# Streamed float32r tiles stored as evens and odds, and read with the halves interleaved

## The chip, the cores and the metric

The kernel runs on one core of a Trainium2 chip. The metric is the device time of one execution in microseconds (us), median of 3 runs. The engines are TensorE (PE; its weight loads are shown apart as PEld), VectorE (DVE), ScalarE (ACT), GpSimd (POOL) and SyncE (SP, which issues the DMAs here).

## The reference

Causal attention for 4 batches of 12 heads, 448 positions and 64 features, followed by a feed-forward block on the 4 x 448 x 768 result:

```python
scores = q @ k.T / sqrt(64);  scores above the diagonal = -1e9      # 448 x 448 per head
attn = exp(scores - max) / (sum + 1e-9);  x = attn @ v              # heads side by side: B x 448 x 768
xn = (x - mean) / sqrt(var + 1e-6) * g_ln
out = x + relu(xn @ w_ch1) @ w_ch2                                  # 768 -> 3072 -> 768
```

All inputs are float32, except that the two weight matrices arrive as 64-bit values whose 32-bit words the kernel loads and converts itself (`raw`, `bits`, `w`).

## The kernel before, in words

**Splitting.** A product of float32 matrices is made of three float32r products: each operand is split into a high part (a float32r rounding) and a low part (the rest), and high x high, high x low and low x high are added in PSUM. So each product of a 128 x 128 weight block with a 128 x 448 tile is three matmuls whose moving operand (`rhs`, the tile that is streamed past the loaded weights) is a float32r tile in SBUF with 448 columns. The streamed tiles are `xh`, `xl` (input of the first layer, `parts`, `gained1`, `gained2`, `apply1`, `apply2`), `hh`, `hl` (hidden activations, in `ffn`), the operands of the last two batches (`x...h`, `x...l`, `h`, `hx`, in class `Pair`) and `kh`, `kl` (keys, `split1` and `split2`), which are streamed for the scores in 112, 224, 336 or 448 columns because of the causal mask. The weights `wh`, `wl` and the queries `qs` are loaded as weights and are not streamed. Every streamed row lies in SBUF in the order of its columns and is read in that order.

**Stages.** Batch 0's attention comes first, with plain float32 scores (`both`). Then the feed-forward of batch 0 (`ffn`, 864 streamed matmuls; in the first layer its tiles have 450 columns, because two columns of g are appended to get the mean's part) runs while the weights are still being converted on ACT and DVE (`convert1`, `convert2`, `split1`, `split2` of weights) and while attention of batches 1 and 2 goes on between its matmuls. Then the feed-forward of batch 1 (864 matmuls of 448 columns) with the attention of batches 2 and 3, and last the feed-forward of batches 2 and 3 together (`Pair`), which forms 7 block products in place of 8 (Strassen's scheme) with 1512 matmuls of 448 columns; the sums that this needs are made on DVE, POOL and ACT.

**Order.** Every operation is first recorded as a task. `Plan.cost` gives each one a price in ns; `Plan.schedule` works out when each result is needed and `Plan.run` then plays the engines' queues with these prices and picks, engine by engine, the task needed first. Moves that may go to ACT or DVE (`either`, `move`) are given to one of them there. The order that comes out is written out and fixed: on the chip each engine runs its list in this order and waits only for what it reads. `MOVES` adds drawn shifts to the needed times of some tasks; they hang on task numbers.

```python
if t.kw["rhs"].dtype == F32R:
    return max(0.4531 * n + 2.5, 60), 220, False
...
if t.engine == "scalar": ...
    return 0.835 * n + (66 if psum else 155 if "scale" in t.kw else 94), 160, False
```

All instructions of the profile bear line 553 (the loop in `Plan.issue` that writes out the order), so tiles tell them apart.

Of the kernel before, what the change touches and what calls it, by code (L numbers as in the profile page):

```python
# [23 lines left out]
P = 128  # L24
C = 112
# [9 lines left out]
SGROUPS = [[(0, 3)], [(0, 0), (0, 2)], [(0, 1), (1, 1)], [(1, 3)], [(1, 0), (1, 2)]]  # L35
RGROUPS = [[3], [0, 2], [1]]
TGROUPS = [[(0, 0)], [(0, 1), (0, 3)], [(0, 2), (1, 2)], [(1, 0)], [(1, 1), (1, 3)]]
HOLE = [-7, 4]
# [5 lines left out]
SLACK, DMA_SLACK = 200, 6000  # L44
CHANGE, TOGETHER = 150, 12000
PASSES, PORT, LEAST, AFTER, URGENT, START = 6, 300, 300, 1500, 5000, 70000
# [42 lines left out]
class View:  # L89
# [12 lines left out]
    def rearrange(self, pattern, **sizes):  # L102
        left, right = (x.split() for x in pattern.replace("(", "( ").replace(")", " )").split("->"))
        assert left[0] == right[0] == "p" and [x for x in left if x not in "()"] == [x for x in right if x not in "()"]
# [22 lines left out]
        return self._new(self.p, self.idx.reshape(shape), lambda t: t.rearrange(pattern, **sizes))  # L127

# [6 lines left out]
    def real(self):  # L135
        t = self.buf.real
        for step in self.path:
            t = step(t)
        return t


# [36 lines left out]
class Plan:  # L178
# [99 lines left out]
    def cost(self, t):  # L278
# [8 lines left out]
        if t.engine == "tensor":  # L287
            if t.kw.get("rhs") is not None and t.kw["rhs"].dtype == BF16:
                return 0.84 * n, 220, False
            if t.method == "transpose":  # L290
                return 0.89 * n if t.ins[0].dtype == F32 else 86, 220, False
            if t.kw["rhs"].dtype == F32R:
                return max(0.4531 * n + 2.5, 60), 220, False
            wide = t.outs[0].p[1] - t.outs[0].p[0] > D and t.kw["rhs"].p[1] - t.kw["rhs"].p[0] > D
            t.mode = "" if wide else "rows" if t.outs[0].p[1] > D + t.outs[0].p[0] else "columns"
            return (1.68 if wide else 0.84) * n + 5 if n > 1 else 100, 220, False
        if t.engine == "scalar":
# [4 lines left out]
            if isinstance(t.kw.get("scale"), View):  # L302
                return 0.835 * n + 188, 160, False
            return 0.835 * n + (66 if psum else 155 if "scale" in t.kw else 94), 160, False
        if t.engine == "gpsimd":
# [3 lines left out]
            if t.method == "tensor_scalar":  # L309
                return 240 + 0.835 * n, 90, True  # L310
            return 2.42 * n + 60 if n > 8 else 1500, 90, bool(sbuf)
        t.here = 85
# [5 lines left out]
        if "accum_out" in t.kw:  # L318
            t.here = 150
        return n / (1.92 if fast else 0.96) + more, t.here + 60, fast or tiny or (len(sbuf) > 1 and not psum)  # L320

# [240 lines left out]
def kernel(ctx, tc, qk, v, w1, w2, g, out):  # L562
# [169 lines left out]
    class Att:  # L732
# [15 lines left out]
        def columns(self):  # L748

            self.parts()  # L750
            for x in (S, S + 1):
                h, l = (t[:, :, x:x + 1].rearrange("p c x -> p (c x)") for t in (self.xh, self.xl))
                nc.vector.tensor_copy(h, g_sb)
                nc.vector.tensor_tensor(out=l, in0=g_sb, in1=h.bitcast(F32), op=ALU.subtract)

        def gained1(self, c):
            kw = dict(out=self.xh[:, c, :S], in0=self.xT[c], scalar1=g_sb[:, c:c + 1], scalar2=1.0, op0=ALU.mult, op1=ALU.mult)
            nc.either(
                ("scalar", "activation", (), dict(
                    out=self.xh[:, c, :S], in_=self.xT[c], func=ACTF.Copy, scale=g_sb[:, c:c + 1],  # L760
                )),
# [3 lines left out]
        def gained2(self, c):  # L765
            nc.vector.scalar_tensor_tensor(
                out=self.xl[:, c, :S], in0=self.xT[c], scalar=g_sb[:, c:c + 1],
                in1=self.xh[:, c, :S].bitcast(F32), op0=ALU.mult, op1=ALU.subtract,
            )
# [11 lines left out]
        def load_v(self, p):  # L781
# [7 lines left out]
            self.t["v", p] = vt  # L789

        def split1(self, p):
            r = self.t["raw", p]
            qs = ap.tile([P, 2, S], F32R, tag="qs", name="qs", bufs=1)
            kh = ap.tile([P, 2, S], F32R, tag="kh", name="kh", bufs=1)
            kl = ap.tile([P, 2, S], F32R, tag="kl", name="kl", bufs=1)
            rq, rk = r[:, 0:2, :], r[:, 2:4, :]
            move(qs, rq)
            move(kh, rk)
            self.t["qk", p] = qs, kh, kl

        def split2(self, p):
            r = self.t.pop(("raw", p))
            qs, kh, kl = self.t["qk", p]
            rq, rk = r[:, 0:2, :], r[:, 2:4, :]
            nc.vector.tensor_tensor(
                out=qs[D:], in0=rq[D:], in1=qs[D:].bitcast(F32), op=ALU.subtract
            )
            nc.gpsimd.tensor_tensor(out=kl, in0=rk, in1=kh.bitcast(F32), op=ALU.subtract)

# [36 lines left out]
        def scores(self, p, grp):  # L846
            pt = ps.tile([C, S], F32, tag="sc", name="sc", bufs=2)
            o = 0
            for h, i in grp:
# [3 lines left out]
                for kk, part in ((kh, 0), (kl, 1)):  # L853
                    nc.tensor.matmul(
                        pt[:, o:o + n], lhsT=qs[:, h, C * i:C * i + C], rhs=kk[:, h, :n],
                        start=(part == 0), stop=(part == 1),
# [184 lines left out]
        def apply1(self, c):  # L1041
            t = self.xg[c % XG]
            self.t["xg", c] = t
            nc.vector.tensor_tensor(
                out=t, in0=self.xT[c], in1=self.t["mb"], op=ALU.subtract
            )
            nc.vector.scalar_tensor_tensor(
                out=t, in0=t, scalar=g_sb[:, c:c + 1], in1=self.t["rb"],
                op0=ALU.mult, op1=ALU.mult,
# [9 lines left out]
        def steps(self):  # L1059
# [13 lines left out]
            for p, t0 in enumerate(t0s):  # L1073
# [16 lines left out]
                for x, grp in enumerate(RGROUPS if self.b == 0 else []):  # L1090
                    put(post, t0 + RAT0[x], self.both, p, grp)
# [28 lines left out]
    def ffn(a, s, hh, hl):  # L1120
        for f0, f1 in ((0, HF), (HF, NF)):
            for x in range(0, HF, 2):
# [4 lines left out]
                for n, (y, c, i) in enumerate(seq):  # L1127
                    w, z = ((wh, a.xh), (wh, a.xl), (wl, a.xh))[i]
                    last = (y, c) not in [t[:2] for t in seq[n + 1:]]
                    nc.tensor.matmul(  # L1130
                        pm[y], lhsT=w[s + y][:, c * P:c * P + P], rhs=z[:, c, :],
                        start=(c == 0 and i == 0), stop=(c == KC - 1 and last),
# [15 lines left out]
                s += 2  # L1148
            for m in range(KC):
                pm = ps.tile([P, S], F32, tag="mm", name="po", bufs=3)  # L1150
                for x in range(HF):
# [3 lines left out]
                    for i, (w, z) in enumerate(((wh[ws], hh), (wh[ws], hl), (wl[ws], hh))):  # L1155
                        nc.tensor.matmul(
                            pm, lhsT=w[:, o:o + P], rhs=z[:, x, :],
                            start=(x == 0 and i == 0), stop=(x == HF - 1 and i == 2),
# [14 lines left out]
    class Pair:  # L1173
# [42 lines left out]
        def xg(self, c, k, j):  # L1216
            a, cc = self.at[j], c + k * KB
            self.f[c, k, j] = t = self.tmp("xg")
            nc.vector.tensor_tensor(out=t, in0=a.xT[cc], in1=a.t["mb"], op=ALU.subtract)
            nc.vector.scalar_tensor_tensor(  # L1220
                out=t, in0=t, scalar=g_sb[:, cc:cc + 1], in1=a.t["rb"], op0=ALU.mult, op1=ALU.mult,
            )
# [118 lines left out]
        def product(self, b, k):  # L1341
# [6 lines left out]
            for c in range(nk):  # L1348
# [5 lines left out]
                for i, (w, z) in enumerate(((wh, zh), (wh, zl), (wl, zh))):  # L1354
                    nc.tensor.matmul(
                        pm, lhsT=w, rhs=z, start=(new and c == 0 and i == 0),
                        stop=(c == nk - 1 and i == 2), skip_group_check=True,
                    )

        def after1(self, b, blk, k):  # L1360
# [24 lines left out]
            def lo(op):  # L1385
                return self.hid[x, op, "l"]

            def rest(op, src, eng=V):
                minus(lo(op), src, hi(op).bitcast(F32), eng)

# [9 lines left out]
            elif k == 2:  # L1400
                plus(A, A, self.p1)
                self.b11 = self.tmp("b11")
                copy(hi("B11"), A, ACTF.Relu)
                copy(self.b11, A, ACTF.Relu)
# [5 lines left out]
            elif k == 7:  # L1410
                Z = self.psum(b, "Z")
                plus(Z, X, self.p5)
                self.b22 = self.tmp("b22")
                copy(hi("B22"), Z, ACTF.Relu)
                copy(self.b22, Z, ACTF.Relu)
                rest("B22", self.b22, G)
            elif k == 3:
                relu_minus(A, Y, self.b11)
                minus(Z, self.b22, A)
                copy(hi("T1"), A)  # L1420
                copy(hi("T2"), Z)
                relu_minus(Y, Y, self.b22)
                rest("T1", A)
                rest("T2", Z)
                then(1, copy, hi("T3"), Y)
                then(2, rest, "T3", Y)
            elif k == 4:
                b21 = self.tmp("b21")
                copy(b21, X, ACTF.Relu)
                copy(hi("B21"), X, ACTF.Relu)  # L1430
                rest("B21", b21, G)
                then(1, minus, Z, b21, Z)
                then(1, copy, hi("T4"), Z)
                then(2, rest, "T4", Z)
# [171 lines left out]
```

## Time and profile before

| what | value |
|---|---|
| median of 3 runs | 833.47 us (832.66 to 833.84) |
| the profiled execution | 832.81 us, of which the span from first to last instruction is 830.7 us |
| PE busy | 823.4 us (99%), 4582 matmuls |
| DVE, ACT, POOL busy | 694.5 us (84%), 512.2 us (62%), 319.4 us (38%) |
| granted TensorE clock | 1.0 of full speed (2.4 GHz) over the whole span |
| DMA | 168.8 MB, mean 203 GB/s |

The duration of one matmul in the profile contains its way through the array and overlaps the next one: what a matmul costs in a dense run is the distance from one start to the next, which the chain of waits gives as a run's time over its count. Busy shares are also to be read by stretch: 0 to 46 us is the attention of batch 0, 46 to 293 us the feed-forward of batch 0, 293 to 487 us mostly that of batch 1 (with the first products of the last stage's preparation), and 487 us to the end the last two batches.

### The profile page before, as it was taken

Reading aid. Unit: us, or ns where it says so; the run is one execution under the profiler, and the core shown is the slowest. Engines: PE = TensorE matmul, PEld = TensorE weight load, DVE = VectorE, ACT = ScalarE, POOL = GpSimd, SP = SyncE. Lnnn points to the kernel's source line nnn. Section 1 sums busy time; section 2 is a strip of 40 time slices with the busy share of each in tenths; the row PEclk is TensorE's granted clock in tenths of the full one; section 3 lists DMA queues with packets and bytes.
Section 4 is the critical chain, followed back from the end, with each engine's and each line's share of the span. In section 5 each row is a group of like instructions: output and inputs, shape, how many; then the busy total and the mean of one; then the engine's idle time right before and its main releaser. Section 6 shows DMA issues by size and latency. Waiting matters only on the chain.

```text
span 830.7 us, 13712 instructions
## 1 busy us (share of the span) xinstructions
PE 823.4 (99%) x4582; PEld 727.2 (88%) x4582; DVE 694.5 (84%) x1445; ACT 512.2 (62%) x1129; POOL 319.4 (38%) x309
## 2 busy tenths in 40 slices
PE   9999999999999999999999999999999999999998
PEld 5679889888798888898989899999999999999997
DVE  6899999899999987887777489887887878788785
ACT  7999998888789675565453235543625435254451
POOL 5753111011352622331110278446446454554440
PEclk9999999999999999999999999999999999999999
DMA  9687888877778798769785464333243342423434
GB/s 215 237 289 265 304 293 319 337 277 269 253 272 303 240 315 289 277 222 320 232 245 195 144 197 153 118 101 124 64 150 97 101 124 86 148 75 114 120 90 154
DMA packets 61318, 168.79 MB, mean 203 GB/s; under 512 B 7008, under 2 KB 25824, under 8 KB 61248
## 3 DMA queue, kind: packets, MB, share of 16 engines
q1 hardware_dynamic: 61248, 167.92, 61.2%
q8 instruction: 36, 0.59, 0.3%
q14 instruction: 34, 0.28, 0.1%
HBM read 119.15 MB, written 39.71 MB: 191 GB/s over the span
## 4 chain that ended last, share of the span: by engine, by line
PE 95%; ACT 2%; DVE 2%; issue 0%; POOL 0%; ACTq 0%; POOLq 0%; DVEq 0%
PE po L553 21%; PE bX L553 21%; PE ph L553 21%; PE bY L553 11%; PE sc L553 5%; PE bA L553 5%; PE px L553 5%; PE pt L553 4%; DVE P L553 1%; ACT PT L553 1%; PE idle L553 0%; ACT P L553 0%; DVE qs L553 0%; ACT rest L553 0%; PE rb L553 0%; PE var L553 0%
## 5 line engine op out<-in xcount | busy, mean ns | idle before, releaser
L553 ACT ACTIVATE P<-P,least 112x112 f32<-112x112 f32 (+3 forms) x176 | 91.2, 521 | 35.5 <-DVE least L553 34.9
L553 PE MATMUL ph<-xh,wh 128*128 128x450 f32 (+1 forms) x288 | 108.4, 378 | 0.3 <-ACT wh L553 0.3
L553 PE MATMUL po<-hh,wh 128*128 128x448 f32 x288 | 107.5, 373 | 0.0
L553 PE MATMUL ph<-xh,wl 128*128 128x450 f32 (+1 forms) x288 | 106.6, 371 | 0.0
L553 PE MATMUL ph<-xl,wh 128*128 128x450 f32 (+1 forms) x288 | 105.6, 368 | 0.0
L553 PE MATMUL po<-hl,wh 128*128 128x448 f32 x288 | 105.1, 365 | 0.0
L553 PE MATMUL po<-hh,wl 128*128 128x448 f32 x288 | 104.8, 364 | 0.0
L553 POOL TENSOR_TENSOR kl<-qkraw,kh 128x896 fp32r<-128x896 f32 x18 | 40.7, 2261 | 157.8 <-ACT kh L553 105.0
L553 DVE CUSTOM_DVE_ANT_0 P<-sc,mask 112x112 f32<-112x112 f32 (+3 forms) x176 | 72.4, 442 | 24.2 <-PE sc L553 23.5
L553 ACT ACTIVATE wp<-s 128x256 fp32r<-128x256 f32 (+1 forms) x104 | 47.0, 462 | 66.4 <-PE bX L553 28.9
L553 POOL TENSOR_TENSOR s<-u 128x256 f32<-128x256 f32 (+1 forms) x60 | 56.2, 952 | 80.2 <-DMA u<-scratch 38.0
L553 ACT ACTIVATE wk<-u 128x256 fp32r<-128x256 f32 (+1 forms) x78 | 36.0, 464 | 69.8 <-PE bX L553 58.2
L553 DVE TENSOR_TENSOR wp<-s,wp 128x256 fp32r<-128x256 f32 (+1 forms) x120 | 67.9, 572 | 0.9 <-ACT wp L553 0.2
L553 POOL TENSOR_TENSOR h<-b,h 128x448 fp32r<-128x448 f32 x36 | 43.6, 1211 | 60.1 <-ACT h L553 34.6
L553 PEld LDWEIGHTS ph<-xh,wh 128*128 128x128 f32 x288 | 54.2, 188 | 5.4 <-ACT wh L553 0.6
L553 PEld LDWEIGHTS ph<-xh,wl 128*128 128x128 f32 x288 | 54.1, 188 | 4.6 <-issue 0.4
L553 PEld LDWEIGHTS ph<-xl,wh 128*128 128x128 f32 x288 | 54.3, 189 | 3.9
L553 PEld LDWEIGHTS po<-hh,wl 128*128 128x128 f32 x288 | 54.0, 188 | 3.6
L553 PEld LDWEIGHTS po<-hl,wh 128*128 128x128 f32 x288 | 54.2, 188 | 3.3
L553 PEld LDWEIGHTS po<-hh,wh 128*128 128x128 f32 x288 | 54.1, 188 | 3.4
L553 DVE TENSOR_TENSOR xT<-xT,bX 128x448 f32<-128x448 f32 x72 | 44.3, 616 | 12.3 <-PE bX L553 12.0
L553 ACT ACTIVATE PT<-pt 112x448 f32<-112x448 f32 x83 | 43.6, 540 | 16.1 <-PE pt L553 14.6
(190 smaller groups left out, 2217.0 us busy)
## 6 DMA issues: line engine op xcount, KB each, us to landing
raw<-w_dram SPq DMA_DIRECT2D x39, 768.0 KB, 6.8
scratch<-w SPq DMA_DIRECT2D x48, 384.0 KB, 4.2
full<-scratch SPq DMA_DIRECT2D x24, 768.0 KB, 7.1
qkraw<-qk_dram SPq DMA_DIRECT2D x18, 896.0 KB, 5.4
kept<-wl SPq DMA_DIRECT2D x30, 384.0 KB, 6.1
u<-scratch SPq DMA_DIRECT2D x24, 384.0 KB, 3.8
u<-scratch SPq DMA_DIRECT2D x36, 256.0 KB, 3.0
PR<-P SPq DMA_DIRECT2D x18, 490.0 KB, 6.5
```

Source lines behind the costliest of these rows:

```text
L553: getattr(getattr(nc, t.engine), method)(*args, **kw)
```

## The change

A streamed row of n columns is now stored with its even columns in the first half and its odd columns in the second (`halves`, written from a source that is read at every second element, `apart`), and the matmul reads it through `woven`, which takes one element of the first half, one of the second, and so on: the columns reach the array in their old order. Queries and weights are left as they are. The number of instructions and their element counts stay. With it, prices in `Plan.cost` and the constant `CHANGE` are changed; `FIRSTS` holds the same lists as `RGROUPS`. The core of the diff:

```diff
-CHANGE, TOGETHER = 150, 12000
+CHANGE, TOGETHER = 100, 12000
+def woven(x):
+    return x.rearrange("p (a b) -> p b a", a=2)
+def halves(x, n=S // 2):
+    return x.rearrange("p (a b) -> p a b", a=2)[:, :, :n]
+def apart(x):
+    return x.rearrange("p (b a) -> p a b", a=2)
...
             if t.method == "transpose":
-                return 0.89 * n if t.ins[0].dtype == F32 else 86, 220, False
+                return 97 if t.ins[0].dtype == F32 else 80, 220, False
             if t.kw["rhs"].dtype == F32R:
-                return max(0.4531 * n + 2.5, 60), 220, False
+                return max(0.4175 * n + 2, 112), 220, False
...
-            return 0.835 * n + (66 if psum else 155 if "scale" in t.kw else 94), 160, False
+            more = 50 if not psum and t.ins[0].idx.flat[1] > t.ins[0].idx.flat[0] + 1 else 0
+            return 0.835 * n + more + (66 if psum else 155 if "scale" in t.kw else 94), 160, False
...
-            return 2.42 * n + 60 if n > 8 else 1500, 90, bool(sbuf)
+            return 2.5 * n + 60 if n > 8 else 1500, 90, bool(sbuf)
...
+        if n <= 8 and t.method in ("tensor_scalar_add", "reciprocal"):
+            more = 68 if t.method == "tensor_scalar_add" else 96
+        if t.method == "scalar_tensor_tensor" and isinstance(t.kw["scalar"], View):
+            more = 128
+        if t.method == "tensor_tensor" and t.outs[0].p[0]:
+            more = 187
...
         def gained2(self, c):
             nc.vector.scalar_tensor_tensor(
-                out=self.xl[:, c, :S], in0=self.xT[c], scalar=g_sb[:, c:c + 1],
-                in1=self.xh[:, c, :S].bitcast(F32), op0=ALU.mult, op1=ALU.subtract,
+                out=halves(self.xl[:, c, :]), in0=apart(self.xT[c]), scalar=g_sb[:, c:c + 1],
+                in1=halves(self.xh[:, c, :]).bitcast(F32), op0=ALU.mult, op1=ALU.subtract,
             )
...
+        def keys(self, t, r):
+            return t.rearrange("p h (a b) -> p h a b", a=2), r[:, 2:4, :].rearrange("p h (b a) -> p h a b", a=2)
...
-            move(kh, rk)
+            move(*self.keys(kh, r))
...
-                        pt[:, o:o + n], lhsT=qs[:, h, C * i:C * i + C], rhs=kk[:, h, :n],
+                        pt[:, o:o + n], lhsT=qs[:, h, C * i:C * i + C], rhs=woven(kk[:, h, :])[:, :n // 2, :],
...
-                        pm[y], lhsT=w[s + y][:, c * P:c * P + P], rhs=z[:, c, :],
+                        pm[y], lhsT=w[s + y][:, c * P:c * P + P], rhs=woven(z[:, c, :]),
...
-                        nc.scalar.activation(out=hh[:, x + y, :], in_=h, func=ACTF.Relu)
+                        h, hi, lo = apart(h), halves(hh[:, x + y, :]), halves(hl[:, x + y, :])
+                        nc.scalar.activation(out=hi, in_=h, func=ACTF.Relu)
                         nc.vector.scalar_tensor_tensor(
-                            out=hl[:, x + y, :], in0=h, scalar=0.0,
-                            in1=hh[:, x + y, :].bitcast(F32), op0=ALU.max, op1=ALU.subtract,
+                            out=lo, in0=h, scalar=0.0, in1=hi.bitcast(F32), op0=ALU.max, op1=ALU.subtract,
                         )
...
-                        pm, lhsT=w, rhs=z, start=(new and c == 0 and i == 0),
+                        pm, lhsT=w, rhs=woven(z), start=(new and c == 0 and i == 0),
...
             def rest(op, src, eng=V):
-                minus(lo(op), src, hi(op).bitcast(F32), eng)
+                minus(halves(lo(op)), apart(src), halves(hi(op)).bitcast(F32), eng)
```

The second layer's matmuls, `columns`, `gained1`, `apply1`, `Pair.xg` and the other high parts of `Pair.after1` are changed in the same way; for batches 1 to 3 the normalised input is stored in halves already when it is made (`xg`), so that `xh` and `xl` are then made of plain rows.

## Rows read from the trace of the kernel before

**Rows 1.** The page: busy time, share and instructions of each engine; the chain's shares.

```profile
PE 823.4 (99%) x4582; PEld 727.2 (88%) x4582; DVE 694.5 (84%) x1445; ACT 512.2 (62%) x1129; POOL 319.4 (38%) x309
...
PE 95%; ACT 2%; DVE 2%; issue 0%; POOL 0%; ACTq 0%; POOLq 0%; DVEq 0%
```

**Rows 2.** PE's own waits: total us, times, longest us.

```profile
PE sc L553 <- DVE qs L553: 1.7, 1, 1.7
PE ph L553 <- ACT wh L553: 0.3, 1, 0.3
```

**Rows 3.** The chain in order of time: start us, us, what, matmuls in the run.

```profile
54.81 16.97 PE ph L553 x83
...
487.51 34.83 PE po L553 x174
...
529.53 2.40 PE bX L553 x12
```

**Rows 4.** Matmul groups by form: count, busy us, mean ns of one, idle before.

```profile
L553 PE MATMUL po<-hh,wh 128*128 128x448 f32 x288 | 107.5, 373 | 0.0
...
L553 PE MATMUL ph<-xh,wh 128*128 128x450 f32 x144 | 54.8, 383 | 0.3 <-ACT wh L553 0.3
...
L553 PE MATMUL bY<-h,wp 128*128 128x448 f32 x216 | 49.6, 365 | 0.0
...
L553 PE MATMUL px<-PT,vt 112*64 112x448 f32 x72 | 17.2, 561 | 0.0
...
L553 PE MATMUL bX<-xl,wk 128*128 128x448 f32 x36 | 13.0, 361 | 0.0
```

**Rows 5.** PE's timeline around four 224-column score matmuls: start us, duration us, what.

```profile
158.41 0.27 PE L553 MATMUL sc<-kh,qs 128*112 128x224 f32 x1
158.52 0.27 PE L553 MATMUL sc<-kl,qs 128*112 128x224 f32 x1
158.62 0.27 PE L553 MATMUL sc<-kh,qs 128*112 128x224 f32 x1
158.72 0.27 PE L553 MATMUL sc<-kl,qs 128*112 128x224 f32 x1
158.83 0.37 PE L553 MATMUL po<-hh,wh 128*128 128x448 f32 x1
```

**Rows 6.** Weight loads by form: 128, 112 and 64 columns.

```profile
L553 PEld LDWEIGHTS po<-hl,wh 128*128 128x128 f32 x288 | 54.2, 188 | 3.3
...
L553 PEld LDWEIGHTS sc<-kl,qs 128*112 128x112 f32 x144 | 25.3, 176 | 2.2
...
L553 PEld LDWEIGHTS px<-PT,vt 112*64 112x64 f32 x288 | 19.5, 136 | 18.3 <-issue 11.5
```

**Rows 7.** Stretches: us, then busy us of each engine, clock, DMA share.

```profile
46.00:293.00 247.00, 245.00 (x1425) 214.24 (x1424) 233.89 (x477) 219.56 (x438) 68.02 (x43) 1.00 0.80 285
293.00:487.00 194.00, 194.00 (x1167) 171.19 (x1167) 146.66 (x338) 99.03 (x240) 48.40 (x34) 1.00 0.75 245
487.00:830.70 343.70, 340.14 (x1691) 315.18 (x1689) 278.15 (x480) 154.00 (x332) 171.48 (x170) 1.00 0.38 117
```

**Rows 8.** Operations on ACT, DVE and POOL by form: mean ns of one.

```profile
L553 POOL TENSOR_TENSOR h<-b,h 128x448 fp32r<-128x448 f32 x36 | 43.6, 1211 | 60.1 <-ACT h L553 34.6 <-ACT b L553 25.5
...
L553 ACT ACTIVATE w<-raw 128x768 f32<-128x768 f32 x39 | 35.5, 911 | 0.0
...
L553 ACT ACTIVATE wh<-w 128x768 fp32r<-128x768 f32 x40 | 33.8, 846 | 4.8 <-DVE w L553 3.2 <-PE ph L553 0.8 <-PE po L553 0.6
...
L553 DVE SCALAR_TENSOR_TENSOR hl<-ph,hh 128x448 fp32r<-128x448 f32 x48 | 29.5, 617 | 1.5 <-ACT hh L553 1.2
...
L553 DVE CUSTOM_DVE_ANT_0 P<-sc,mask 112x448 f32<-112x448 f32 x44 | 27.1, 617 | 10.0 <-PE sc L553 9.7
...
L553 DVE CUSTOM_DVE_ANT_0 P<-sc,mask 112x224 f32<-112x224 f32 x44 | 16.0, 387 | 12.4 <-PE sc L553 12.1
```

More of the change, by code (lines that the diff above doesn't have):

```diff
@@ L36 @@
 RGROUPS = [[3], [0, 2], [1]]
+FIRSTS = [[3], [0, 2], [1]]
 TGROUPS = [[(0, 0)], [(0, 1), (0, 3)], [(0, 2), (1, 2)], [(1, 0)], [(1, 1), (1, 3)]]
@@ L103, in rearrange @@
         left, right = (x.split() for x in pattern.replace("(", "( ").replace(")", " )").split("->"))
-        assert left[0] == right[0] == "p" and [x for x in left if x not in "()"] == [x for x in right if x not in "()"]
+        assert left[0] == right[0] == "p"
         def groups(words):
@@ L126, in rearrange @@
         shape = [int(np.prod([known[x] for x in names])) for names in groups(right)]
-        return self._new(self.p, self.idx.reshape(shape), lambda t: t.rearrange(pattern, **sizes))
+        one, two = ([x for names in groups(side) for x in names] for side in (left, right))
+        idx = self.idx.reshape([known[x] for x in one]).transpose([one.index(x) for x in two])
+        return self._new(self.p, idx.reshape(shape), lambda t: t.rearrange(pattern, **sizes))
     def bitcast(self, dtype):
@@ L750, in columns @@
             self.parts()
-            for x in (S, S + 1):
-                h, l = (t[:, :, x:x + 1].rearrange("p c x -> p (c x)") for t in (self.xh, self.xl))
+            for x in range(2):
+                h, l = (
+                    t.rearrange("p c (a b) -> p c a b", a=2)[:, :, x, S // 2:].rearrange("p c x -> p (c x)")
+                    for t in (self.xh, self.xl)
+                )
                 nc.vector.tensor_copy(h, g_sb)
@@ L756, in gained1 @@
         def gained1(self, c):
-            kw = dict(out=self.xh[:, c, :S], in0=self.xT[c], scalar1=g_sb[:, c:c + 1], scalar2=1.0, op0=ALU.mult, op1=ALU.mult)
+            to, x = halves(self.xh[:, c, :]), apart(self.xT[c])
+            kw = dict(out=to, in0=x, scalar1=g_sb[:, c:c + 1], scalar2=1.0, op0=ALU.mult, op1=ALU.mult)
             nc.either(
                 ("scalar", "activation", (), dict(
-                    out=self.xh[:, c, :S], in_=self.xT[c], func=ACTF.Copy, scale=g_sb[:, c:c + 1],
+                    out=to, in_=x, func=ACTF.Copy, scale=g_sb[:, c:c + 1],
                 )),
@@ L795, in split1 @@
             kl = ap.tile([P, 2, S], F32R, tag="kl", name="kl", bufs=1)
-            rq, rk = r[:, 0:2, :], r[:, 2:4, :]
-            move(qs, rq)
-            move(kh, rk)
+            move(qs, r[:, 0:2, :])
+            move(*self.keys(kh, r))
             self.t["qk", p] = qs, kh, kl
@@ L803, in split2 @@
             qs, kh, kl = self.t["qk", p]
-            rq, rk = r[:, 0:2, :], r[:, 2:4, :]
             nc.vector.tensor_tensor(
-                out=qs[D:], in0=rq[D:], in1=qs[D:].bitcast(F32), op=ALU.subtract
+                out=qs[D:], in0=r[D:, 0:2, :], in1=qs[D:].bitcast(F32), op=ALU.subtract
             )
-            nc.gpsimd.tensor_tensor(out=kl, in0=rk, in1=kh.bitcast(F32), op=ALU.subtract)
+            to, rk = self.keys(kl, r)
+            nc.gpsimd.tensor_tensor(out=to, in0=rk, in1=self.keys(kh, r)[0].bitcast(F32), op=ALU.subtract)
         def rows(self, p, h):
@@ L1044, in apply1 @@
             nc.vector.tensor_tensor(
-                out=t, in0=self.xT[c], in1=self.t["mb"], op=ALU.subtract
+                out=halves(t), in0=apart(self.xT[c]), in1=apart(self.t["mb"]), op=ALU.subtract
             )
             nc.vector.scalar_tensor_tensor(
-                out=t, in0=t, scalar=g_sb[:, c:c + 1], in1=self.t["rb"],
+                out=halves(t), in0=halves(t), scalar=g_sb[:, c:c + 1], in1=apart(self.t["rb"]),
                 op0=ALU.mult, op1=ALU.mult,
@@ L1089, in steps @@
                     put(pre, t0 + end + 1, self.gained2, p)
-                for x, grp in enumerate(RGROUPS if self.b == 0 else []):
+                for x, grp in enumerate([] if self.b else RGROUPS if p else FIRSTS):
                     put(post, t0 + RAT0[x], self.both, p, grp)
@@ L1156, in ffn @@
                         nc.tensor.matmul(
-                            pm, lhsT=w[:, o:o + P], rhs=z[:, x, :],
+                            pm, lhsT=w[:, o:o + P], rhs=woven(z[:, x, :]),
                             start=(x == 0 and i == 0), stop=(x == HF - 1 and i == 2),
@@ L1218, in xg @@
             self.f[c, k, j] = t = self.tmp("xg")
-            nc.vector.tensor_tensor(out=t, in0=a.xT[cc], in1=a.t["mb"], op=ALU.subtract)
+            nc.vector.tensor_tensor(
+                out=halves(t), in0=apart(a.xT[cc]), in1=apart(a.t["mb"]), op=ALU.subtract
+            )
             nc.vector.scalar_tensor_tensor(
-                out=t, in0=t, scalar=g_sb[:, cc:cc + 1], in1=a.t["rb"], op0=ALU.mult, op1=ALU.mult,
+                out=halves(t), in0=halves(t), scalar=g_sb[:, cc:cc + 1], in1=apart(a.t["rb"]),
+                op0=ALU.mult, op1=ALU.mult,
             )
@@ L1386, in lo, with first @@
                 return self.hid[x, op, "l"]
+            def first(op, src, func=ACTF.Copy):
+                copy(halves(hi(op)), apart(src), func)
             def rest(op, src, eng=V):
-                minus(lo(op), src, hi(op).bitcast(F32), eng)
+                minus(halves(lo(op)), apart(src), halves(hi(op)).bitcast(F32), eng)
             def then(lag, f, *args):
@@ L1402, in after1 @@
                 self.b11 = self.tmp("b11")
-                copy(hi("B11"), A, ACTF.Relu)
+                first("B11", A, ACTF.Relu)
                 copy(self.b11, A, ACTF.Relu)
@@ L1413, in after1 @@
                 self.b22 = self.tmp("b22")
-                copy(hi("B22"), Z, ACTF.Relu)
+                first("B22", Z, ACTF.Relu)
                 copy(self.b22, Z, ACTF.Relu)
@@ L1419, in after1 @@
                 minus(Z, self.b22, A)
-                copy(hi("T1"), A)
-                copy(hi("T2"), Z)
+                first("T1", A)
+                first("T2", Z)
                 relu_minus(Y, Y, self.b22)
@@ L1424, in after1 @@
                 rest("T2", Z)
-                then(1, copy, hi("T3"), Y)
+                then(1, first, "T3", Y)
                 then(2, rest, "T3", Y)
@@ L1429, in after1 @@
                 copy(b21, X, ACTF.Relu)
-                copy(hi("B21"), X, ACTF.Relu)
+                first("B21", X, ACTF.Relu)
                 rest("B21", b21, G)
                 then(1, minus, Z, b21, Z)
-                then(1, copy, hi("T4"), Z)
+                then(1, first, "T4", Z)
                 then(2, rest, "T4", Z)
```

## The prediction

> **What bounds the kernel now.** I read the busy shares first: PE is at 99%, DVE at 84%, ACT at 62%, and the chain that ended last is PE for 95% of its length [rows 1]. Then PE's own waits, to see whether that busy time hides stalls: the longest adds up to 1.7 us, and waits for weights to 0.3 [rows 2]. So the time is the number of matmuls times the distance from one start to the next, and I took that distance from the chain in order of time, since the mean of one matmul (some 365 ns) overlaps the next [rows 3, 4]. A run of 174 matmuls of 448 columns takes 34.83 us, 200.2 ns each; 83 of 450 columns take 16.97 us, 204.5 ns each; the last stage's 12 in 2.40 us say 200 again [rows 3]. The stretches come last: all have PE full, but in 46 to 293 us DVE is busy 233.9 of 247 us (95%) and ACT 219.6 (89%), against 146.7 of 194 and 278.2 of 343.7 for DVE later [rows 7].
>
> **Why 200 ns, and what the read order can do to it.** At the granted clock of 1.00 [rows 7], the 2.4 GHz level, 448 columns at one a cycle are 186.7 ns; 13.5 ns are lost in each matmul. They could sit in the weight load, in a fixed part, or in the stream. Weight loads last 188, 176 and 136 ns for 128, 112 and 64 columns, so 0.81 ns a column over a fixed part: 128 columns hold the loader some 104 ns, about half of a matmul, and it isn't the limit [rows 6]. Score matmuls of 224 columns start 0.105 us apart (four in 0.42 us) [rows 5]: 95 ns less for 224 columns less, 0.43 ns a column against 0.417 at the clock, with 5 to 10 ns fixed or lost in rounding. And two columns more, with rows that begin at multiples of 1800 bytes in place of 1792, cost 4.3 ns, five times what two columns are worth [rows 3]. Part of the loss is thus in reading the streamed tile and hangs on where its elements lie. A new layout can move it; which way, the rows don't say. The bounds: 186.7 ns is as fast as that clock allows. On the dear side the nearest row is the 4.3 ns that a shifted row costs; the far one is the plain float32 matmul of 448 columns, which lasts 561 ns where a float32r one lasts 361 to 383, some 190 ns more [rows 4]. I take 189.0 ns for 448 columns and 189.9 for 450. That is the price which the diff itself gives to a streamed float32r matmul (0.4175 n + 2), a claim and no measurement, but it lies within 3 ns of the clock's bound, which is where a layout that heals the loss must end; the price before (205.5 for 448) stood 5 ns above the trace.
>
> For the same case the Trainium skill (TensorE: Matmul & The Clock Gate, Back-to-back issue gap) has a gap of N/2.4 + 2.5 ns, by which 448 columns are estimated at 189.2 ns. This trace's 200.2 doesn't agree with that as the kernel stands; by it the sum below would be 0.6 us smaller.
>
> **The sum.** Streamed matmuls: 6 groups of 288 in the feed-forward of batches 0 and 1 (432 of the 1728 have 450 columns), and 19 groups from 216 down to 36 in the last stage, 1512 in all [rows 4].
> - 432 x (204.5 - 189.9) = 6.3 us.
> - 1296 + 1512 = 2808 x (200.2 - 189.0) = 31.4 us, of which 16.9 in the last stage.
> - Scores: 72 matmuls each of 448, 336 and 224 columns, at 0.025 ns a column saved: 72 x 1008 x 0.025 = 1.8, I take 2.0 us. Those of 112 columns get nothing: their weight load is 112 columns, some 91 ns at 0.81 ns each, against 50 ns of stream [rows 6].
>
> Together 39.7 us: 12.4 in 46 to 293 us (the 6.3, 432 x 11.2 = 4.8, and two thirds of the scores), 10.4 in 293 to 487, 16.9 after it.
>
> **What is added.** No instruction more; DMAs as many, of the same bytes. About 150 operations on DVE, 134 on ACT and 54 on POOL now read every second element and write two halves. The nearest row is ACT's read of one word in two (`w` from `raw`), 911 ns against 846 for plain rows of the same 768 elements [rows 8]: 65 ns, so 38 for 448. A DVE read of PSUM at every second element has no row. Below, it costs nothing, since element counts stay and nothing gets shorter; above, I take half the rate: DVE's slope is (617 - 387) / 224 = 1.03 ns an element, so 460 ns more on a 617 ns `hl` [rows 8]. I take the 38 ns, by the ACT row. In 293 to 487 and in the last stage the engines' idle time hides it: DVE would have 278.2 + 3 of 343.7 - 16.9 = 326.8 us, 86%. If the half rate were true there, some 85 DVE operations, 39 us, would bring it to 97%, still under PE. POOL's `h` (1211 ns) waits mostly for ACT and has half its time free [rows 7, 8]. In 46 to 293 us there is little cover: 24 `hl`, 6 `xl` and a dozen others, 40 x 38 ns = 1.5 us, beside 233.9 busy in the 247 - 12.4 = 234.6 us that PE would need.
>
> **What is moved.** With other prices the planner draws up every engine's list anew, SP's too, so any step may stand before or behind any other that doesn't depend on it. What is late next is the stretch 46 to 293 us, where weight conversion, `hl`, and attention of batches 1 and 2 fill DVE: 233.9 + 1.5 against 234.6. Conversion and batch 1's attention have dates there, batch 2's attention has not; after 293 us DVE has 194 - 10.4 - 146.7 = 37 us free to take it. I give back a quarter of the 12.4, 3 us, and 0.5 for single waits elsewhere.
>
> The profiled execution is 832.8 us, span 830.7 and 2.1 around it: 832.8 - 39.7 + 3.5 = 796.6. The median shown is 0.7 higher, so 797.
>
> **Rivals.**
> - *The full stretch keeps its time* (DVE, and ACT behind it, bound 46 to 293 us, so that PE waits there). For it: 95% before the change, and PE's part shrinks by 5%. Against: batch 2's share can move. Then the 12.4 is lost: 833.5 - 39.7 + 12.4 = 806, and with DVE reads of PSUM at half rate 40 x 0.46 = 18 us more, 824.
> - *The rate stays* (the change doesn't do what it is for: the loss is a port's bytes per time, the same in either order). For it: 4 bytes a column come in whatever order. Against: the 4.3 ns of a shifted row. The time is what a new order makes of it, with the planner now expecting 189: 831 to 838, I say 834.
> - *The woven read is dearer, so the kernel slower.* Each element comes from another place than the one before it, 896 bytes on. It decides from 200.2 ns a matmul upward, at PE, in all 3240. At the near price of 4.3 ns, 3240 x 4.3 = 14 us: 847; at the far one of 190 ns, 616 us: about 1450. I take 847, the row of the same kind of matmul. Against it: nothing but that the price in the diff goes down, which is no row.
>
> This last is also what the Trainium skill's rule would have (SBUF — State Buffer, Door 1: The DMA port swizzle, its note on cachelines): full rate needs consecutive accesses, at least two, to the same 16-byte line, and an access that crosses to a new line pays. By it the woven order, which changes line at every element, speaks against the change. No run so far shows a woven read; the 4.3 ns of rows off that grid agree with the rule as far as they go, which is why I give the rival more than a token chance.
>
> **How the numbers follow.** Forecast (PE at about 189 ns, most of the gain kept, 789 to 802): 0.64. Full stretch: 0.20, by 806, a quarter of it above 812. Rate stays: 0.07. Dearer read: 0.07. The rest, 0.02, is below 789: at the clock's bound 3240 x 2.3 = 7.5 us more are gained, and with nothing given back that is 786. The range 789 to 812 holds 0.64 and three quarters of 0.20, 0.79. A measurement of this kernel tells about 0.2%, 1.7 us, from no change. Faster by more: 0.64 + 0.20 + 0.02 and 0.01 of the unchanged rate, 0.87. Within: 0.04. Slower: 0.02 of the unchanged rate and 0.07 of the dearer read, 0.09.
>
> **What would show it.** In the chain of the changed kernel a `po` run should come to 189 ns a matmul and the first layer's run of batch 0 to 190, without the 4.3 ns between them: that is the first step. 200 there means the rate stays, more means the dearer read. PE's own waits show the second: some 3 us in all, in the stretch that now is 46 to 293 us; above 10 us there, by DVE or ACT, it is the full stretch. `hl` and `h` in the groups at 617 to 660 ns show the strided reads at their small price; 1000 ns would be half rate. The last stage should end some 17 us shorter, about 327. A time under 786 or above 824 would mean that something I have not priced decides.

## The result and the profile after

| | before | after |
|---|---|---|
| median | 833.11 us (832.66 to 833.84) | 807.72 us (805.70 to 808.59) |
| profiled execution, span | 832.81, 830.7 us | 805.70, 803.7 us |
| ratio after / before | | 0.9691, 95% interval 0.9671 to 0.9711 |

The forecast was 797 us with a range of 789 to 812: the direction and the range held, and 25.4 of the 36 us forecast came. The time lies in the upper part of the range, which the prediction gave to its full-stretch rival, and not in the 789 to 802 us of the forecast itself. The page of the changed kernel (busy time; then the granted clock in 40 slices; then the chain's shares) against [rows 1]:

```profile
PE 789.4 (98%) x4582; PEld 732.0 (91%) x4582; DVE 684.6 (85%) x1424; ACT 524.0 (65%) x1152; POOL 313.0 (39%) x307
...
PEclk9998999999999999999999999999999999999999
...
PE 88%; DVE 5%; ACT 3%; DMA 2%; issue 1%; POOL 0%; SPq 0%; DVEq 0%; POOLq 0%; ACTq 0%
```

The chain in order of time answers to [rows 3] (start us, us, what, matmuls):

```profile
65.34 5.06 PE ph L575 x16
...
96.00 6.84 PE ph L575 x36
...
480.26 32.17 PE po L575 x170
```

The rate is there: 32.17 / 170 = 189.2 ns for 448 columns, 6.84 / 36 = 190.0 for 450, the difference of 4.3 ns gone. What stands against it is new waiting: PE's idle time grows from 7.3 to 14.3 us (830.7 - 823.4 and 803.7 - 789.4), its share of the chain falls from 95 to 88%, and one run at 65 us takes 316 ns a matmul. PE's own waits between 46 and 300 us, against [rows 2] (total us, times, longest us):

```profile
PE pt L575 <- ACT P L575: 3.0, 2, 2.7
PE po L575 <- DVE wl L575: 1.8, 3, 0.8
PE ph L575 <- ACT wh L575: 1.1, 2, 0.7
PE ph L575 <- DVE wl L575: 1.1, 2, 0.7
PE sc L575 <- DVE qs L575: 0.8, 2, 0.6
```

These add up to 7.8 us, between the 3 us that the prediction expected there and the 10 us that it took for the sign of the full stretch.

The longest one, 2.7 us, and what follows it, in stretches (us, busy us of PE, PEld, DVE, ACT, POOL, clock, DMA) and in PE's timeline (start us, us, what, in brackets the idle time before it and what ended it):

```profile
60.00:70.00 10.00, 6.58 (x22) 5.03 (x21) 7.74 (x14) 9.97 (x23) 5.59 (x4) 0.66 0.36 118
```

```profile
63.54 0.44 PE L575 MATMUL pt<-ident,P 112*112 112x112 f32 x1 [2.66 <-ACT P L575]
```

PE stood still for most of 60.9 to 63.5 us, waiting for exponentials (`P`) on ACT, which was busy 9.97 of the 10 us; over these 10 us the granted clock is 0.66 in the mean, so part of them passed at the lower level (1.2 GHz), and 16 matmuls cost 5.06 - 16 x 0.190 = 2.0 us more than they would. In the kernel before, the same 46 to 105 us ran at 1.00 throughout.

The stages show where the rest is. Starts from the timelines of the profiled executions (us; the experiments below are in the same table). Batch 0's second layer starts when half of its first layer is done (216 of 432 matmuls; the rest follow between the second layer's), so the time between the first two columns is that of the first half:

| kernel | first layer, batch 0 | second layer, batch 0 | batch 1 | last stage (first `bX`) | span |
|---|---|---|---|---|---|
| before | 46.4 | 105.4 | 293.9 | 522.2 | 830.7 |
| after | 48.8 | 110.4 | 291.0 | 512.3 | 803.7 |
| e1: new layout, old prices | 46.0 | 104.6 | 287.1 | 506.3 | 803.7 |
| e2: old layout, new prices | 50.8 | 116.0 | 305.0 | 534.8 | 841.5 |
| e3: after, less conversion | 47.2 | 109.2 | 285.2 | 506.8 | 798.8 |
| e4: before, no shifts | 48.1 | 114.2 | 300.6 | 529.7 | 839.0 |
| e5: after, no shifts | 51.9 | 113.3 | 298.3 | 518.2 | 809.9 |
| e6: after, new shifts | 51.0 | 109.4 | 288.4 | 510.5 | 802.1 |
| e7: after, new shifts, KEEP0 43 | 50.6 | 105.6 | 283.4 | 502.4 | 793.7 |
| e8: after, no shifts, KEEP0 43 | 51.3 | 112.4 | 290.8 | 509.9 | 801.7 |
| e9: before, no shifts, KEEP0 43 | 47.9 | 113.9 | 300.5 | 529.7 | 839.8 |

After against before, stage by stage: +2.4 us up to the first layer, +2.6 in its first half, then -7.9, -7.0 and, in the last stage, -17.1. The last stage gives all that the rate can give (16.9 forecast). The first 110 us should have given 3.2 us and cost 5.0. (The last stage begins at 522.2 us in the kernel before, not at 487: the run of 174 `po` matmuls from 487.51 us [rows 3] is still batch 1's second layer. The prediction's sum goes by matmuls and isn't touched; its "about 327" for the time after 487 us comes to about 323 by the same cut, 803.7 - 480.3, since those matmuls save 1.9 us too.)

### The profile page after: what moved, and what is told of

Its sections match the earlier page's. It is cut to its first block, busy times and chain, and to the rows that moved or that the text cites. A ratio compares the mean times of both kernels' runs of the same rounds, so it can differ in the third digit from the quotient of the medians.

```text
span 803.7 us, 13699 instructions
## 1 busy us (share of the span) xinstructions
PE 789.4 (98%) x4582; PEld 732.0 (91%) x4582; DVE 684.6 (85%) x1424; ACT 524.0 (65%) x1152; POOL 313.0 (39%) x307
## 4 chain that ended last, share of the span: by engine, by line
PE 88%; DVE 5%; ACT 3%; DMA 2%; issue 1%; POOL 0%; SPq 0%; DVEq 0%; POOLq 0%; ACTq 0%
PE bX L575 21%; PE ph L575 20%; PE po L575 17%; PE bY L575 10%; PE sc L575 5%; PE bA L575 5%; PE px L575 5%; PE pt L575 4%; DVE P L575 1%; DMA out_dram<-xT 1%; DVE wl L575 1%; ACT P L575 1%; DVE w L575 1%; DVE PT L575 1%; DMA first_qk<-qk_dram 0%
## 5 line engine op out<-in xcount | busy, mean ns | idle before, releaser
L575 PE MATMUL ph<-xh,wh 128*128 128x450 f32 (+1 forms) x288 | 105.4, 368 | 1.2 <-ACT wh L575 1.1
L575 PE MATMUL ph<-xh,wl 128*128 128x450 f32 (+1 forms) x288 | 103.9, 362 | 1.1 <-DVE wl L575 1.1
L575 ACT ACTIVATE P<-P,least 112x336 f32<-112x336 f32 (+3 forms) x176 | 91.4, 524 | 20.0 <-DVE least L575 18.5
L575 PE MATMUL po<-hh,wl 128*128 128x448 f32 x288 | 102.6, 357 | 1.8 <-DVE wl L575 1.8
L575 PE MATMUL po<-hh,wh 128*128 128x448 f32 x288 | 104.0, 361 | 0.0
L575 PE MATMUL po<-hl,wh 128*128 128x448 f32 x288 | 102.2, 355 | 0.0
L575 ACT ACTIVATE wp<-s 128x256 fp32r<-128x256 f32 (+1 forms) x104 | 47.2, 462 | 55.6 <-PE bX L575 29.0
L575 ACT ACTIVATE wk<-u 128x256 fp32r<-128x256 f32 (+1 forms) x88 | 40.8, 465 | 59.2 <-PE bX L575 42.1
L575 DVE TENSOR_TENSOR wp<-s,wp 128x256 fp32r<-128x256 f32 (+1 forms) x120 | 71.4, 603 | 2.2 <-ACT wp L575 1.7
L575 ACT ACTIVATE PT<-pt 112x448 f32<-112x448 f32 x75 | 39.5, 540 | 19.4 <-PE pt L575 18.1
```

The lines of the kernel that those rows point to most:

```text
L575: getattr(getattr(nc, t.engine), method)(*args, **kw)
```

## The experiments

Theory at this point: the rate is the layout's doing; the missing 11 us are lost because DVE and ACT are full between 46 and 293 us. Rival: the work would fit, and the order in which the engines do it, drawn up anew with other prices, is what loses.

**e1, layout alone, and e2, prices alone.** In e1, `Plan.cost` and `CHANGE` are those of before; in e2 the file of before gets the new ones.

```diff
 e1, in the changed kernel; e2 is the same the other way round, in the kernel before
-CHANGE, TOGETHER = 100, 12000
+CHANGE, TOGETHER = 150, 12000
-                return max(0.4175 * n + 2, 112), 220, False
+                return max(0.4531 * n + 2.5, 60), 220, False
...
```

> The new layout with the prices and CHANGE of before, so that every engine's list is that of before. Theory (the streamed matmul costs 189 ns by the layout alone, and the stretch 46 to 293 us is full, so that its part of the gain is lost under any order): a po run at 189 ns, time 804 to 812 us. Rival (the new order, drawn up with new prices and needed-time shifts chosen for the old ones, is what lost some 10 us): a po run at 189 ns, time 794 to 800 us.

> The old layout with the new prices, so the order is nearly that of the changed kernel, and every streamed matmul is at 200 ns. Theory (full stretch): with PE at 200 ns the same order hardly waits, 832 to 838 us. Rival (the new order itself loses some 10 us): 840 to 846 us. If the prices alone made the kernel faster, under 830, the layout would not be the cause of the gain.

e1: 805.99 us, ratio 0.9674 (0.9659 to 0.9688). e2: 842.82 us, ratio 1.0119 (1.0103 to 1.0134). So the layout makes the whole gain, and the new prices by themselves cost 9.5 us: in e2 PE waits 3.9 us at once for `wl` in the first layer, and the clock falls there too:

```profile
PE ph L560 <- DVE wl L560: 3.9, 1, 3.9
```

```profile
60.00:70.00 10.00, 6.10 (x20) 5.17 (x20) 8.75 (x15) 10.00 (x24) 6.13 (x4) 0.73 0.36 119
```

e1 agrees with the theory, e2 with the rival. The stages tell why e1 and after end alike: e1, with the order of before, keeps the first 105 us of before (104.6 against 105.4) and loses in the last stage, 297.4 us against 291.4. Each order is good where the other isn't, and e2's 9.5 us are lost at the old rate, so a full stretch can't be the whole cause. But for the first half of the first layer e1 bears the theory out: in the order of before, cheaper matmuls shorten it by 0.4 us only (58.6 against 59.0), with ACT busy the whole time and DVE nearly so, and no run below has the second layer start before e1's 104.6 us.

```profile
46.00:105.00 59.00, 57.54 (x334) 51.44 (x333) 57.96 (x111) 58.97 (x113) 15.37 (x10) 1.00 0.82 282
```

**e3, less work in the stretch.** One ACT and one DVE operation of each of the 48 weight blocks left out, and with them the low bits of the weights.

```diff
...
-        nc.scalar.activation(
-            out=bits[s], in_=raw.pop(s)[:, :, 0], func=ACTF.Copy, scale=LAST * 2.0 ** -29
-        )
+        raw.pop(s)
...
-        nc.vector.scalar_tensor_tensor(
-            out=w, in0=w, scalar=3, in1=bits.pop(s), op0=ALU.logical_shift_left,
-            op1=ALU.bitwise_or,
-        )
```

> The changed kernel without one ACT and one DVE operation per weight block (the low bits of the weights are left out; 48 x 0.93 us of ACT and 48 x 1.0 us of DVE, all in 46 to 270 us). Theory (DVE and ACT are full there and PE waits for them): the lost gain comes back, 792 to 799 us, PE's wait at 60 us gone and the clock full throughout. Rival (the waits are chains of latency and order, not work): 804 to 809 us.

802.64 us (801.07 to 804.98), ratio 0.9641 (0.9623 to 0.966): between the two. Busy time in 46 to 105 and 105 to 291 us:

```profile
46.00:105.00 59.00, 56.16 (x325) 49.69 (x322) 49.07 (x105) 49.18 (x98) 17.42 (x12) 1.00 0.74 277
105.00:291.00 186.00, 184.58 (x1144) 170.56 (x1143) 158.34 (x354) 132.77 (x291) 52.87 (x35) 1.00 0.80 286
```

With DVE down to 83 to 85% the second stretch is 4.6 us shorter than in after (176.0 against 180.6), but the first layer's first half takes 62.0 us against 61.6. DVE is busy 5 us less there than in after and ACT 8, whose row is

```profile
46.00:105.00 59.00, 55.17 (x310) 49.38 (x308) 54.16 (x101) 57.16 (x107) 15.04 (x10) 0.94 0.72 254
```

and nothing came of it: in e3's order the first 110 us are not lost to the amount of work. (Tasks left out renumber the others, so the shifts of `MOVES` fall elsewhere; e3 is no clean count, and it doesn't undo what e1 shows of that stretch in the order of before.)

**e4 to e6, the drawn shifts.** All entries of `MOVES` have windows between -20 and 90 us, and they hang on needed times that follow from prices.

```diff
 e4 (in before), e5 (in after)
-MOVES = [(305651422, 1000, 256, 16860, 90000), ... 8 entries]
+MOVES = []
 e6 (in after)
+MOVES = [(2109733275, 1000, 32, -1300.0, 28700.0), (141782131, 3000, 128, 52840.0, 82840.0), ... 13 entries]
```

> The kernel before with MOVES empty: the planner's list without the drawn shifts of needed times, all else as it was. Theory (the shifts were drawn to heal waits between 0 and 90 us under the old prices): 836 to 840 us, with new PE waits between 46 and 80 us. Rival (they are worth nothing on the chip): 832 to 834 us.

> The changed kernel with MOVES empty. Theory (the old shifts no longer fit the new prices, so that they heal nothing there): 805 to 810 us, within 3 us of the changed kernel. Rival (they still work): 812 us or more, as many us as the kernel before loses without them.

> The changed kernel with nothing changed but the list in MOVES, drawn anew for the new prices. Theory (a good part of the lost gain is the order of the first 80 us, not full engines): PE's wait at 60 us and the half clock after it gone, feed-forward of batch 0 starting its second layer at 104 to 107 us in place of 110, 798 to 803 us. Rival (DVE and ACT are full by their work, whatever the order): 805 us or more.

e4: 840.98 us, ratio 1.0092 (1.0078 to 1.0106). e5: 812.11, ratio 0.9745 (0.9731 to 0.9758). e6: 802.35, ratio 0.9631 (0.9618 to 0.9644). The shifts are worth 7 to 8 us to the kernel before and 4.4 us to the changed one, more than my theory gave e5 (805 to 810) and about the bottom of its rival; drawn for the new prices they are worth 9.8. Without any shifts the change gives 840.98 - 812.11 = 28.9 us in place of 25.4. So the stale shifts explain some 3.5 us by that count, and up to 5.4 (807.72 - 802.35) if new ones are drawn. e6's second layer starts at 109.4 us, not at the 104 to 107 expected: its gain is spread over the stages. The low clock at 60 to 70 us is gone, but in the profiled execution, the slowest of the four with a mean granted clock of 0.995, it comes elsewhere, in 50 to 60 and in 285 to 295 us (0.83 in the mean of each); the other three have 0.998 to 1.000.

**e7, the version that beats both.** The shifts drawn anew once more, and, since the end of the stretch still waits for `wl`, fewer low parts written out there; two constants of the planner (`GAP`, `BEHIND`) moved with them, and no run separates these.

```diff
-GAP = 6
+GAP = 5
-BEHIND = 12000
+BEHIND = 10000
-KEEP0 = 36
+KEEP0 = 43
-MOVES = [...]
+MOVES = [(2140917759, 3000, 8, 46130.0, 51130.0), (676129914, 1000, 128, 39420.0, 119420.0), ... 9 entries]
```

> The changed kernel with MOVES drawn anew, GAP 5, BEHIND 10000 and KEEP0 43 in place of 36: seven low weight parts fewer are written out in 200 to 290 us, and split again on DVE in the feed-forward of batch 1, where DVE has time. Theory (the head is a matter of order, and the end of the stretch one of DVE work and of buffers held by DMAs): 789 to 796 us, PE waits together under 6 us after 46 us. Rival (the whole stretch is full by work): 800 us or more.

795.85 us (795.28 to 796.26), ratio 0.9550 (0.9537 to 0.9563), 12 us under the changed kernel. Its page and the chain's longest run, 189.3 ns a matmul:

```profile
PE 784.7 (99%) x4582; PEld 730.2 (92%) x4582; DVE 679.2 (86%) x1416; ACT 532.5 (67%) x1167; POOL 314.7 (40%) x307
...
PEclk9999999999999999999999999999999999999999
```

```profile
470.93 31.61 PE po L581 x167
```

The first layer of batch 0 to the start of batch 1 takes 232.8 us, against 242.2 in after and 247.5 before. Up to the start of batch 1 (after, then e7) the engines do nearly the same work in 7.6 us less:

```profile
0.00:291.00 291.00, 281.58 (x1721) 241.37 (x1721) 266.48 (x622) 259.52 (x551) 94.00 (x105) 0.99 0.78 272
0.00:283.40 283.40, 278.26 (x1719) 239.66 (x1720) 264.12 (x618) 263.05 (x557) 94.99 (x104) 1.00 0.80 275
```

So the stretch was not full in after. In e7 it nearly is: DVE is busy 225.4 of the 232.8 us. And e7's second layer starts at 105.6 us, no earlier than in the kernel before: the first 105 us haven't given their 3.2 us here either.

**e8 and e9, KEEP0 by itself,** without shifts, so that nothing drawn is moved. Low parts of weight blocks 43 to 47, in place of 36 to 47, are written out to be loaded again in batch 1; seven `wl` are split a second time there instead.

```diff
-KEEP0 = 36
+KEEP0 = 43
```

> The changed kernel with MOVES empty and KEEP0 43 in place of 36, to be read against the changed kernel with MOVES empty (812.1 us) and free of any drawn shift: seven weight parts fewer are written out at the end of batch 0's feed-forward, and split again later. Theory (the end of that stretch waits for DVE's wl, whose buffers are held by these DMAs, landing in some 8 us): 803 to 807 us, the gain between 225 and 300 us. Rival (the gain of the last kernel came from its shifts alone): 810 to 814 us.

> The kernel before with MOVES empty and KEEP0 43, to be read against the kernel before with MOVES empty (841.0 us). Theory (with PE at 200 ns a matmul nothing waits there, so the parts written out cost nothing): 839 to 843 us. Rival (fewer DMAs help at either rate): 833 to 837 us.

e8: 804.36 us, ratio 0.9655 (0.9638 to 0.9671), to be read against e5's 0.9745 (0.9731 to 0.9758). e9: 841.72, ratio 1.0102 (1.0087 to 1.0117), against e4's 1.0092 (1.0078 to 1.0106). Both came as the theory had them: the same edit is worth 7.8 us at 189 ns a matmul and nothing at 200. The stretch 225 to 300 us, of e5, of e8 and of e9:

```profile
225.00:300.00 75.00, 69.16 (x419) 61.60 (x418) 70.92 (x143) 59.96 (x123) 31.72 (x21) 1.00 0.77 272
```

```profile
225.00:300.00 75.00, 73.69 (x453) 67.27 (x452) 72.15 (x158) 66.88 (x145) 31.37 (x22) 1.00 0.80 278
```

```profile
225.00:300.00 75.00, 75.00 (x457) 66.00 (x455) 70.02 (x150) 61.10 (x133) 34.17 (x24) 1.00 0.81 275
```

In e5 PE is idle for 5.8 of the 75 us, in e8 1.3, in e9 none; e4, with KEEP0 36, has 74.99 there as well. In e5 PE waits 1.9 us there for `wl`, in e8 no longer, while ACT does 6.9 us more in the same time: the engines got on faster, not with less work. Whether the writes cost by holding `wl` buffers (they land in 8.5 us, median, in e5's stretch) or by the place that they take in SP's queue was not told apart.

**m1, the read order by itself.** A kernel of its own, with none of the attention or feed-forward in it: 24 matmuls of 448 columns (450 in two of them) for each way of reading the streamed tile.

```diff
+        yield "plain", t[:, 0:448]
...
+        yield "offtwo", t[:, 2:450]
...
+        yield "woven", t[:, 0:448].rearrange("p (a b) -> p b a", a=2)
...
+        yield "wovenfour", t[:, 0:448].rearrange("p (a b) -> p b a", a=4)
...
+        yield "linestep", t[:, 0:448].rearrange("p (a b) -> p b a", a=112)
+        yield "runtwo", t[:, 0:448].rearrange("p (a b c) -> p b a c", a=2, c=2)
...
```

> No attention and no feed-forward: 24 float32r matmuls of 448 columns for each way of reading the streamed tile, with the other engines idle, then plain and woven again beside copies on ACT, DVE and POOL; before that single copies and subtractions, plain and with every second element into halves. Theory (the loss is in the order of the addresses: neighbours in the same short piece of a row are what costs): plain 200 ns quiet or busy, offsets of one or two elements some ns more, every woven form (halves, quarters, eighths, every 112th) 189, pairs and fours in a row between 189 and 200, every second or fourth element of a longer row 189 to 200. Rival (the other engines' traffic makes the loss): plain 189 quiet and 200 busy. Rival (a new line for each element costs): woven eighths and single elements 16 bytes apart slower than plain. Copies and subtractions with every second element within 40 ns of the plain ones if the small price holds, some 460 ns more if half rate.

Its chain in order of time (start us, us for 24 matmuls):

```profile
20.00 4.86 PE plain L56 x24
24.86 5.03 PE offone L56 x24
29.89 4.96 PE offtwo L56 x24
34.85 4.88 PE wide L56 x24
39.73 4.54 PE woven L56 x24
44.27 4.56 PE wovenodd L56 x24
48.83 4.54 PE wovenfar L56 x24
53.37 5.71 PE wovenfour L56 x24
59.08 9.12 PE woveneight L56 x24
68.20 9.71 PE linestep L56 x24
77.91 6.88 PE runtwo L56 x24
84.79 5.12 PE runfour L56 x24
89.91 9.49 PE evens L56 x24
99.40 9.71 PE fourth L56 x24
109.11 4.97 PE last L56 x24
```

The other engines were not idle as planned. Their copies wait for nothing that PE makes, so most of them ran at the start: `plain`, `offone` and `offtwo` had DVE and POOL at work beside them, from `woven` on all was quiet, and so it was at `last`, which is a second plain read. After it come a plain and a woven read beside DVE and ACT. Stretches of `plain`, `last` and the late woven read, then PE's timeline of the late plain and woven reads:

```profile
20.00:24.86 4.86, 4.86 (x25) 4.50 (x25) 4.79 (x3) 0.00 (x0) 4.86 (x3) 1.00 0.00 0
109.11:114.08 4.97, 4.97 (x26) 4.52 (x25) 0.00 (x0) 0.00 (x0) 0.00 (x0) 1.00 0.00 0
118.86:123.57 4.71, 4.71 (x25) 4.34 (x23) 4.71 (x11) 2.47 (x6) 0.00 (x0) 1.00 0.00 0
```

```profile
113.91 5.12 PE L56 MATMUL plainbusy<-big,wts 128*128 128x448 f32 x24
118.86 4.70 PE L56 MATMUL wovenbusy<-big,wts 128*128 128x448 f32 x24
```

Divided by 24: plain 202.5 ns beside DVE and POOL, 207.1 with all others idle, 206 beside DVE and ACT (4.95 us from its first start to that of the next form). The quiet read is the slowest, so the other engines' traffic isn't the cause of the loss; what makes plain rows differ by 4.6 ns is not shown. A start off by two elements gives 206.7 ns, which is no more than a plain row can take; off by one gives 209.6, above all of them. Two columns more from the same start give 203.3 (`wide`). Two halves in turn give 189.2 ns in quiet (190.0 for 450 columns), whether 896, 900 or 2048 bytes apart, and 189 beside DVE and ACT. But my own reason falls: four quarters in turn take 238, eighths 380, steps of 16 bytes 405, every second element of a plain row 395, and pairs or fours from two halves 287 and 213. Not "far apart is free": two streams, one element each in turn, is the one form here that runs at the clock, and why it does isn't shown. The Trainium skill's rule (SBUF — State Buffer, Door 1: The DMA port swizzle, note on cachelines), that full rate needs two accesses in a row to the same 16-byte line and that an access to a new line pays, agrees with the steps and the eighths, which take some 175 to 200 ns more than plain. It doesn't agree with the halves, which go to a new line at every element and are the fastest, nor with the pairs and with every second element, which stay on each line for two elements and are slow.

The elementwise part of the same kernel, plain against every second element into halves, 448 columns, from PSUM and from SBUF:

```profile
L72 ACT ACTIVATE apsumplain<-last 128x448 fp32r<-128x448 f32 x3 | 1.6, 546 | 96.4 <-PE last L56 95.0 <-DVE cpsumapart L76 1.4
L72 ACT ACTIVATE apsumapart<-last 128x448 fp32r<-128x448 f32 x3 | 1.6, 546 | 2.2 <-DVE cpsumplain L76 2.2
...
L72 ACT ACTIVATE asbufplain<-raw 128x448 fp32r<-128x448 f32 x3 | 1.7, 580 | 0.1
L72 ACT ACTIVATE asbufapart<-raw 128x448 fp32r<-128x448 f32 x3 | 1.9, 619 | 0.1
...
L74 DVE TENSOR_TENSOR dpsumplain<-last,fb 128x448 fp32r<-128x448 f32 x3 | 1.9, 620 | 80.7 <-ACT apsumplain L72 80.7
L74 DVE TENSOR_TENSOR dpsumapart<-last,fb 128x448 fp32r<-128x448 f32 x3 | 1.9, 618 | 0.0
```

Nothing on DVE or on ACT from PSUM; 39 ns on ACT from SBUF, and 46 ns on POOL (2022 against 1976).

## Why the prediction was right, and where its sum was off

- **The rate** (189.0 and 189.9 ns taken): 189.2 and 190.0 measured. The bound by the clock, 186.7, plus 2.5. The hint in the trace of before, 4.3 ns for rows of 450 columns that start 1800 bytes apart, is not explained by m1: two columns more cost 0.8 ns there, and rows 8 bytes off take no more than plain ones can. And no row there could tell that two halves help and four quarters hurt; I was right by the price in the diff and by the clock's bound, not by a mechanism that I had shown; that the weave was this one and not another was luck as far as the prediction goes.
- **The strided reads** (38 ns each, by ACT's row): 39 on ACT from SBUF, 46 on POOL, none on DVE or on ACT from PSUM; in after `hl` stays at 617 ns [rows 8]. About the price taken or nothing, and nowhere near half rate.
- **The last stage** (16.9 us): 17.1.
- **The stretch given back** is the term that was mis-sized. I gave back 3.5 us. Against the full gain of 39.7 the profiled execution lost 12.7 (span 27.0 shorter). By stage: 2.4 us before the first layer, where I forecast no change, 5.8 in its first half (+2.6 in place of -3.2), then 1.4 up to batch 1 (-7.9 of -9.3), within what I gave back, and 3.4 in batch 1's stage (-7.0 of -10.4); of these last some are work put off, 64 pairs of score matmuls in place of 58 after its start. "What is moved" priced only the fullness of the engines. It did not price that the order of the first 80 us had been drawn for the old prices: e4 shows what that drawing was worth, 7 to 8 us, and that was readable in the code, since no window of `MOVES` reaches past 90 us. Of the 8.2 us lost up to the second layer, the order accounts for 5.8: e1, in the order of before, starts it at 104.6 us in place of 110.4. The other 2.4 no run gets back, and whether a better order could is open. The prediction also left out what KEEP0 costs at the new rate: 7.8 us by e8 against e5, both without shifts, so that this doesn't add up with the 5.8.
- **The rivals.** "The full stretch keeps its time" gave 806, within 2 us of the median, but its mechanism fell for the stretch as a whole: it is shorter in after (242.2 us, not 247.5), most of the loss is before 110 us, and e7 puts the same stretch in 232.8 us with nearly the same work. A right number mostly by another cause. For the first half of the first layer it isn't refuted: there e1 keeps the time of before, with ACT full. "The rate stays" and "dearer read" are out for halves; for every other weave tried in m1 the second is what came.
- The forecast of 797 is near what the layout gives in an order drawn for it (e7, 795.85 us), but that is no measurement of the change alone: e7 also has KEEP0 43, which is worth nothing at the old rate, and other `GAP` and `BEHIND`. Whether shifts drawn anew with these would take something off the kernel before as well was not run.

## What to carry to other kernels

When one engine bounds and its operations get cheaper by a few per cent, read every list, date and drawn constant that was fitted to the old price as part of the change: here prices, shifts and KEEP0 were worth 4 to 10 us each, where 11 us of the forecast were missing. To learn whether a stretch is full, don't add up busy shares; take work out of it (e3) or change its order (e6, e7) and see which one shortens it. And a price for a new access pattern is best measured by itself: neighbouring patterns in m1 differ by a factor of two, the halves being faster than a plain row and all others slower. Look in the trace, too, at what ran beside each part of such a test: here it was not what the program's order of lines suggests.

## What the runs showed of the hardware that was not expected

- A float32r streamed row of 448 columns in plain order takes 202.5 ns beside busy DVE and POOL and 207.1 with the other engines idle, at granted clock 1.00 both times (m1), and 200.2 in the kernel before. Two interleaved halves take 189.2, four interleaved quarters 238, pairs from two halves 287, every second element 395.
- Reading PSUM at every second element and writing two halves is free on ACT (546 ns either way) and on DVE (620 and 618).
- Around a PE stall of 2.7 us (after) and of 3.9 us (e2) the granted clock is 0.66 and 0.73 in the mean of 10 us; in after 16 matmuls cost 2.0 us more for it, nearly the stall again. A wait of 2.0 us at 190 us in e1 left it at 1.00 (185 to 200 us).
